# Late stores on SyncE, and spectral-gradient groups between the rows of x's gradient

## The chip, the cores and the metric

The kernel runs on one core of one Trainium2 chip. The metric is the device time of one execution in microseconds (us), the median of several runs. "The span" is the stretch from the first to the last record of one profiled execution. The names of the profile: PE is TensorE (its matmuls; PEld are its weight loads), DVE is VectorE, ACT is ScalarE, POOL is GpSimd, SP is SyncE. A trailing q (SPq, POOLq) means the engine's instruction queue, which also issues transfers.

## The reference

Forward and backward pass of one block in bfloat16, with x of 2048 x 448: a spectral layer, then a token-mixing MLP, each behind a layernorm and with a residual.

```python
h  = x + irfft2(rfft2(layernorm(x)) * (w_r + 1j * w_i))
z  = layernorm(layernorm(h))
h2 = h + (gelu(z.T @ w1 + b1) @ w2 + b2).T
# returned: h2, and for grad_out the gradients of x, w_r, w_i, w1, b1, w2, b2
out_0 = h2
out_1, out_2, out_3 = grad_x, grad_w_r, grad_w_i      # 2048x448, 2048x225, 2048x225
out_4, out_5 = grad_w1, grad_b1                       # 2048x1792, 1792
out_6, out_7 = grad_w2, grad_b2                       # 1792x2048, 2048
```

## The kernel before

The sequence (2048) is cut into 16 rows of 128 partitions, the hidden size F (1792) into 14 blocks of 128. The Fourier transforms are matmuls with tables, with sums and differences on DVE between them.

The program is not written in its final order. Every operation is given to a planner (`Plan.op`) with the engines that may run it, a cost, the buffers it reads and writes, and a level (`pl.boost`). `Plan.order` then places the operations engine by engine: of those that can start it takes the one with the highest priority (the longest chain behind it plus the level). Buffers come from rings of fixed depth; `w4` (5 deep) holds the output rows of out_4 and out_6, `k1` (8) small tiles such as gx, `hx` (3) the loaded rows of x, `e4` (3) the products of the spectral gradients, and `ps` the 8 PSUM banks, of which each kind of use may hold a limited number (`mm` 4, `sb` 4, `mw` 8). Loads on SP have a fixed order. A store (`st`, line 513; its DMA is line 515) goes to POOL unless `on="S"` puts it on SP; an operation waits in its engine's queue, in order, until its data are there.

What is at work in the last 60 us:

- Rows of x's gradient, h = 0 to 15. `ifft_rows` (line 966) makes a row of the inverse transform: four matmuls of `ab` with `di` (tile ps_sb), an ACT copy `odd`, two DVE operations `eo` (lines 977, 979), three matmuls with `kinv` (a "kinv triple"), an ACT copy and two DVE operations `y` (lines 992, 994). `norm_back` (line 1249) is the backward layernorm: a DVE row total (line 1262) and `nm` (line 1274), an ACT `v` (line 1267), DVE `junk` (line 1285) and `gx` (line 1288). Line 1373 stores gx to out_1.
- Outer products of out_6 (14 of them), then of out_4 (16, h = 0 to 15): `outer` (line 1379) makes four banks with 12 whole-array matmuls and four half-array matmuls, the "tails", which run two at a time. Up to `EARLY` (line 1377) the kind is `mm`, with the tails between the second and third bank; from there on the kind is `mw`, with the tails last for even h and first for odd h, so that neighbours share a change of array shape. `copy` evicts each bank as a CAST into `s` (line 523 on ACT, line 525 on DVE). Line 1437 stores a row of out_4 (448 KB); the last row is stored in four pieces of 112 KB (line 1441).
- The spectral gradients out_2 and out_3, in five groups (`JG`, of 4, 3, 3, 3 and 3 planes). `cmul` (line 887) makes two products `t_r` and `t_i` (line 896) and two sums into `ds` (lines 903, 905), all on DVE, and four stores follow. A soft dependency (line 1426) keeps a group's products behind the gx of a given row.

Of the kernel before, what the change touches and what calls it, by code (L numbers as in the profile page):

```python
# [18 lines left out]
P = 128  # L19
S = 2048  # L20
D = 448
DF = 225
F = 1792
# [360 lines left out]
def _act(n, base=0.045):  # L384
    return base + 0.855e-3 * n, base + 0.11 + 0.855e-3 * n
# [6 lines left out]
def on_act(n, base=0.045):  # L392
    return [("ACT", *_act(n, base))]


def on_dve(n, per=1.04e-3, base=0.066):
    return [("DVE", *_dve(n, per, base))]
# [14 lines left out]
def evict(n):  # L412
    return on_act(n) + on_dve(n)


def mm(*cols):
    t = sum(0.002 + 0.4215e-3 * max(n, 120) for n in cols)
    return [("PE", t, t + 0.07)]
# [3 lines left out]
def kernel(  # L422
# [40 lines left out]
    pl = Plan(nc, tc, rings)  # L463
# [14 lines left out]
    def big(i, shape, name, dtype=BF16):  # L478
        return pl.buf(f"X{i}", shape, name, dtype)

    def k1(shape, name, dtype=BF16):
        return pl.buf("k1", shape, name, dtype)

    def bank(kind, shape, dtype=F32):
        return pl.buf("ps", shape, "ps_" + kind, dtype, kind)
# [27 lines left out]
    def st(out, in_, size, r, w=(), issue=0.6, on="P", order=None, rate=0.335):  # L513
        def go(e, on):
            e.dma_start(out=out() if callable(out) else out, in_=in_())  # L515

        pl.op([("POOL", issue, issue) if on == "P" else ("SP", 0.45, 0.45)], go, r=r, w=w,
              dma=(size, rate * 1e6, False), order=order)

    def copy(alts, out, in_, r, w):  # L520
        def go(e, on):
            if on == "ACT":
                e.copy(out=out(), in_=in_())  # L523
            else:
                e.tensor_copy(out=out(), in_=in_())

        pl.op(alts, go, r=r, w=w)

    def matmuls(bk, calls, r, cost=None, modes=("whole", "cols")):


        def go(e, on):
            for n, out, lhsT, rhs, start, stop in calls:
                out, lhsT = out(), lhsT()
                if not split or op.mode != "cols":
                    e.matmul(out, lhsT=lhsT, rhs=rhs(), start=start, stop=stop)  # L536
                    continue
                m, each = out.shape[0], int(np.prod(lhsT.shape[2:]))
                for a, b_ in ((0, 64), (64, m)):
                    e.matmul(out[a:b_], lhsT=lhsT[:, a // each:b_ // each], rhs=rhs(), start=start, stop=stop)  # L540

        split = cost is None
        op = pl.op(cost or mm(*[c[0] for c in calls]), go, r=r, w=bk if isinstance(bk, list) else [bk], modes=modes)
        return op

    def rows(ap):
        return ap.rearrange("(q h) d -> q h d", h=NT)
# [339 lines left out]
    def cmul(a, b, out, j0, j1, conj):  # L887
        n = j1 - j0
        js = range(j0, j1)
        t_r = pl.buf("e4", [P, 2, n, DF], "t_r")  # L890
        t_i = pl.buf("e4", [P, 2, n, DF], "t_i")
        ra = [(a, j) for j in js]
        rb = [(b, j) for j in js] if b is not w_now[0] else [b]

        def times(t, c):
            pl.op(tt(2 * n * DF), lambda e, on: e.tensor_tensor(
                out=t[:], in0=a[:, :, j0:j1, :], in1=b[:, c:c + 1, j0:j1, :].broadcast_to([P, 2, n, DF]),
                op=ALU.mult), r=ra + rb, w=[t])

        times(t_r, 0)  # L900
        times(t_i, 1)
        (o_r, o_i), ow = out(j0, j1)
        pl.op(tt(n * DF), lambda e, on: e.tensor_tensor(out=o_r(), in0=t_r[:, 0], in1=t_i[:, 1],
                                                       op=ALU.add if conj else ALU.subtract), r=[t_r, t_i], w=ow(0))
        pl.op(tt(n * DF), lambda e, on: e.tensor_tensor(out=o_i(), in0=t_r[:, 1], in1=t_i[:, 0],
                                                       op=ALU.subtract if conj else ALU.add), r=[t_r, t_i], w=ow(1))
# [3 lines left out]
    def in_place(b):  # L910
        def out(j0, j1):
            return (((lambda: b[:, 0, j0:j1, :]), (lambda: b[:, 1, j0:j1, :])),
                    lambda c: [(b, (c, j)) for j in range(j0, j1)])
        return out
# [201 lines left out]
    for j in range(NFB):  # L1116
        wc, o = w1c[j]
# [31 lines left out]
        if j % 4 == 3 or j == NFB - 1:  # L1149
            j0 = j - j % 4  # L1150
# [186 lines left out]
    hlnT = big(1, [P, 4, S], "hlnT")  # L1337
    du_t = big(8, [P, 4, F], "du_t")
# [17 lines left out]
    ds = big(4, [P, 2, NJ, DF], "ds")  # L1356
# [7 lines left out]
    gx_op = []  # L1364
    for h in range(NT):
        with grouped():
            py = ifft_rows(ab2, di1, h, y2)
            g = h // 2
            gx = k1([P, D], "gx")
            norm_back((y2, h % 7), lambda g=g, h=h: xr[g][:, h % 2, :], (xr[g], h % 2), h, nx,  # L1370
                      lambda h=h: dh[:, h, :], lambda gx=gx: gx[:], ((dh, h), gx))
        gx_op.append(pl.ops[-1])
        st(rows(out_1[0])[:, h, :], lambda gx=gx: gx[:], P * D * 2, [gx])

    behind, EARLY = [], 10

    def outer(kind, a_t, b_t, j, width, dst, turn, evict_):


        bs = [bank(kind, [P, width]) for _ in range(4)]
        held = [(dst, ("held", 0))]
        begins = (lambda n: n < 2) if turn is None else (lambda n: turn == 0)

        def call(n, rows_, c, start, stop):
            return (width, lambda: bs[n][:], lambda: a_t[rows_, c, j * P:(j + 1) * P],
                    lambda: b_t[rows_, c, width * n:width * n + width], start, stop)

        def whole(*ns):  # L1390
            return matmuls(bs[ns[0]:ns[-1] + 1], [call(n, slice(0, P), c, c == 0 and begins(n), c == 2 and not begins(n))
                                                  for n in ns for c in range(3)],
                           [(a_t, (0, i)) for i in range(4)] + [(b_t, (0, n)) for n in ns] + held)

        def tails():
            return matmuls(bs, [call(n + i, (LO, UP)[i], 3, not begins(n), begins(n)) for n in (0, 2) for i in range(2)],
                           [(t, k) for t in (a_t, b_t) for k in (1, 2)] + held, mm(width, width), ("rows",))

        with grouped():
            if turn is None:  # L1400
                os = [whole(0), whole(1), tails(), whole(2), whole(3)]
            elif turn == 0:
                os = [whole(0, 1), whole(2, 3), tails()]
            else:
                os = [tails(), whole(0, 1), whole(2, 3)]
            for o in os:
                if behind:
                    o.soft.add(behind[-1].idx)
                behind.append(o)
            for n in range(4):  # L1410
                copy(evict_, lambda n=n: dst[:, width * n:width * n + width], lambda n=n: bs[n][:], [bs[n]], [(dst, n)])
                pl.ops[-1].level = 300.0

    for j in range(NFB):
# [2 lines left out]
        st(out_6[j * P:(j + 1) * P, :], lambda s6=s6: s6[:], P * S * 2, [s6],  # L1417
           on="S" if j in s6_at else "P", order=s6_at.get(j))

    pl.boost = 0.0  # L1420
    o23 = [o.rearrange("(q b r) k -> b q r k", b=2, r=NJ) for o in (out_2, out_3)]
    for i, (j0, j1) in enumerate(JG):
        at = len(pl.ops)
        cmul(ds, xs, in_place(ds), j0, j1, True)
        for o in pl.ops[at:at + 2]:
            o.soft.add(gx_op[(3, 6, 9, 12, 15)[i]].idx)
        for c in range(2):
            for b_ in range(2):
                st(o23[c][b_, :, j0:j1, :], lambda c=c, b_=b_, j0=j0, j1=j1: ds[64 * b_:64 * b_ + 64, c, j0:j1, :],
                   64 * (j1 - j0) * DF * 2, [(ds, (c, j)) for j in range(j0, j1)], on="S")  # L1430

    pl.boost = 0.0
    for h in range(NT):
        s4 = pl.buf("w4", [P, F], "s4")
        outer(*(("mm",) if h < EARLY else ("mw",)), hlnT, du_t, h, 448, s4, None if h < EARLY else h % 2, on_act(448) if h < 13 else evict(448))
        if h < NT - 1:
            st(rows(out_4)[:, h, :], lambda s4=s4: s4[:], P * F * 2, [s4])
        else:
            for n in range(4):
                sl = slice(448 * n, 448 * n + 448)  # L1440
                st(rows(out_4)[:, h, sl], lambda s4=s4, sl=sl: s4[:, sl], P * 448 * 2, [(s4, n)], on="SPSP"[n])

# [36 lines left out]
```

## Time and profile before

| | |
|---|---|
| median of 3 runs | 340.83 us (340.62 to 341.41) |
| profiled execution: its own time / its span | 340.38 us / 338.49 us |
| granted TensorE clock over the span | 0.987 |
| PE, DVE, ACT, POOL busy | 95%, 79%, 61%, 17% of the span |
| first matmul of out_4 / last matmul's end | 280.06 us / 329.69 us |
| stores issued after 300 us by POOL / SP | 19 / 22 |

Times are counted from the start of the span. An operation's busy time on DVE or ACT overlaps the next one's by some 0.1 us, so a queue of operations is summed by the differences of their starts. A transfer is seen twice: when its engine issues it, and when its landing is counted by a semaphore.

### The profile page before, as it was taken

How to read it: one execution, taken by the hardware profiler on the slowest of the kernel's cores; microseconds unless marked ns; L12 is line 12 of the kernel's file. 1: busy time of each engine (PE TensorE's matmuls, PEld its weight loads, DVE VectorE, ACT ScalarE, POOL GpSimd, SP SyncE). 2: the span in 40 equal slices, each digit the busy share in tenths (PEclk: the TensorE clock that was granted, in tenths of full speed). 3: DMA queues.
4: the chain of work that ended last, by engine and by line, in shares of the span. 5: the costliest groups of instructions: out<-in, count | busy, mean ns of one | idle time of the engine just before them, and what ended most of it. 6: DMA issues, size and time to landing. Idle time of an engine off the chain costs nothing.

```text
span 338.5 us, 6989 instructions
## 1 busy us (share of the span) xinstructions
PE 321.5 (95%) x2543; PEld 175.3 (52%) x2554; DVE 268.2 (79%) x763; ACT 206.4 (61%) x458; POOL 57.1 (17%) x99
## 2 busy tenths in 40 slices
PE   6869999999999999999999999999999999999990
PEld 2537755666655555555555555554555544544440
DVE  5996999898849997062147988789989799999990
ACT  3886744477668774262302222597877899899650
POOL 0000000047530101042150000000001122433320
PEclk9989999999999999999999999999999999999996
DMA  7999899996698999999999999999982245654684
GB/s 232 383 216 231 180 224 252 209 276 210 200 336 216 338 343 253 282 267 306 269 242 241 257 213 227 229 247 260 266 269 115 103 179 220 244 195 186 220 290 147
DMA packets 135807, 81.01 MB, mean 239 GB/s; under 512 B 94396, under 2 KB 128508, under 8 KB 135644
## 3 DMA queue, kind: packets, MB, share of 16 engines
q1 hardware_dynamic: 129708, 57.70, 73.3%
q0 software_dynamic: 6064, 22.85, 18.7%
q8 instruction: 20, 0.33, 0.4%
q14 instruction: 15, 0.12, 0.1%
HBM read 30.98 MB, written 27.08 MB: 172 GB/s over the span
## 4 chain that ended last, share of the span: by engine, by line
PE 68%; DVE 21%; issue 3%; ACT 2%; DMA 2%; SPq 0%; POOL 0%; POOLq 0%; DVEq 0%; ACTq 0%
PE ps_mp L536 25%; PE ps_mm L536 15%; PE ps_mg L536 10%; PE ps_sp L536 6%; PE ps_sb L536 5%; DVE junk L1262 4%; PE ps_mw L536 4%; DVE junk L1285 4%; PE ps_mm L540 2%; DMA w2n<-in_B_w_dram 2%; ACT v L1267 2%; DVE gg L853 2%; DVE u L806 1%; DVE w L806 1%; DVE bs_x L717 1%
## 5 line engine op out<-in xcount | busy, mean ns | idle before, releaser
L523 ACT CAST s<-ps_mm 128x512 bf16<-128x512 f32 (+1 forms) x96 | 50.3, 582 | 6.2 <-PE ps_mm L536 5.3
L536 PE MATMUL ps_mm<-du,w1T 128*128 128x449 bf16 x224 | 43.4, 353 | 0.0
L536 PE MATMUL ps_mp<-hln,w1c 128*128 128x448 bf16 x224 | 42.9, 352 | 0.0
L536 PE MATMUL ps_mp<-gT,w2c 128*128 128x448 bf16 x224 | 42.9, 352 | 0.0
L536 PE MATMUL ps_mm<-goT,g_t 128*128 128x512 bf16 (+1 forms) x180 | 40.0, 380 | 0.9 <-issue 0.5
L536 PE MATMUL ps_mg<-go_n,w2T 128*128 128x448 bf16 x180 | 40.7, 364 | 0.0
L1267 ACT ACTIVATE v<-ps_mm,nm,rn_h 128x448 f32<-128x448 f32 x16 | 11.6, 725 | 41.0 <-DVE nm L1280 41.0
L536 PEld LDWEIGHTS <-w1T 128*128 128x128 bf16 x224 | 21.7, 97 | 21.0
L536 PEld LDWEIGHTS <-w2c 128*128 128x128 bf16 x224 | 21.9, 98 | 20.5
L536 PEld LDWEIGHTS <-w1c 128*128 128x128 bf16 x224 | 21.9, 98 | 20.3
L536 PEld LDWEIGHTS <-hlnT 128*128 128x128 bf16 (+1 forms) x256 | 19.5, 97 | 21.3 <-issue 6.7
L536 PE MATMUL ps_mm<-du_t,hlnT 128*128 128x448 bf16 (+1 forms) x160 | 30.4, 353 | 0.0
L536 PEld LDWEIGHTS <-w2T 128*128 128x128 bf16 x180 | 16.4, 100 | 13.3 <-issue 2.2
L536 PEld LDWEIGHTS <-g_t 128*128 128x128 bf16 (+1 forms) x191 | 13.3, 97 | 17.0 <-issue 6.0
L1224 DVE SCALAR_TENSOR_TENSOR h<-ps_mp,b2c,hr 128x448 bf16<-128x448 f32 x16 | 9.9, 678 | 14.4 <-PE ps_mp L536 13.8
L515 POOL DMA_DIRECT2D out_dram<-s x25 | 13.5, 542 | 45.0 <-ACT s L523 26.8
L1132 DVE SCALAR_TENSOR_TENSOR ge<-ge 128x448 bf16<-128x448 bf16 x14 | 8.7, 621 | 13.4 <-ACT ge L1130 13.4
L1128 ACT ACTIVATE ge<-ps_mp,b1c 128x448 bf16<-128x448 f32 x14 | 8.8, 626 | 14.1 <-PE ps_mp L536 12.8
L536 PE MATMUL ps_mw<-du_t,hlnT 128*128 128x448 bf16 (+1 forms) x96 | 16.7, 353 | 0.0
L1262 DVE CUSTOM_DVE_ANT_0 junk<-v,hln 128x448 bf16<-128x448 f32 x16 | 10.0, 623 | 7.8 <-ACT v L1267 7.7
L515 POOL DMA_DIRECT2D hn_d<-x x4 | 2.4, 589 | 75.2 <-DVE rn_h L732 71.4
L1231 ACT ACTIVATE gb2j<-go_r 128x448 bf16<-128x448 bf16 x16 | 9.2, 576 | 9.5 <-DMA go_r<-in_grad_out_dram 9.1
(156 smaller groups left out, 634.8 us busy)
## 6 DMA issues: line engine op xcount, KB each, us to landing
w2c<-in_B_w_dram SPq DMA_DIRECT2D x8, 896.0 KB, 9.9
out_dram<-s POOLq DMA_DIRECT2D x15, 448.0 KB, 2.9
w1c<-in_B_w_dram SPq DMA_DIRECT2D x6, 1024.0 KB, 11.9
out_dram<-s POOLq DMA_DIRECT2D x8, 512.0 KB, 3.0
out_dram<-s SPq DMA_DIRECT2D x6, 512.0 KB, 4.5
x<-in_A_x_dram SPq DMA_DIRECT2D x4, 448.0 KB, 7.0
go_n<-in_grad_out_dram SPq DMA_DIRECT2D x2, 896.0 KB, 10.6
hn_d<-x POOLq DMA_DIRECT2D x4, 448.0 KB, 5.2
```

The costliest lines, as they stand in the source:

```text
L515: e.dma_start(out=out() if callable(out) else out, in_=in_())
L523: e.copy(out=out(), in_=in_())
L536: e.matmul(out, lhsT=lhsT, rhs=rhs(), start=start, stop=stop)
L540: e.matmul(out[a:b_], lhsT=lhsT[:, a // each:b_ // each], rhs=rhs(), start=start, stop=stop)
L806: pl.op(tt(4 * n), lambda e, on: e.tensor_tensor(out=out(), in0=in0(), in1=in1(), op=op), r=r, w=w_)
L1128: gop([("ACT", 0.516, 0.62)], [pu, b1c], [uf], lambda e, g, j=j, pu=pu: e.activation(out=g(uf), in_=pu[:, 0:D], func=ACT.Identity, bias=b1 ...
L1132: gop(stt, [q_, uf], [zz], lambda e, g: e.scalar_tensor_tensor(out=g(zz), in0=g(q_), scalar=6.0 * GELU_C, in1=g(uf), op0=ALU.add, op1=ALU. ...
L1224: pl.op([("DVE", 0.595, 0.68)], lambda e, on, t=t, p2=p2, h2=h2: e.scalar_tensor_tensor(out=h2[:], in0=p2[:, 0:D], scalar=b2c[:, t:t + 1], ...
L1231: pl.op([("ACT", 0.70, 0.80)], lambda e, on, h=h: e.activation(out=gb2j[:], in_=go_r[:, h, :], func=ACT.Copy, accum_out=gb2[:, h:h + 1]), ...
L1262: pl.op([("DVE", 0.605, 0.73)], lambda e, on: e.tensor_tensor_reduce(out=junk[:], in0=src(), in1=xhat(), scale=scale(), scalar=0.0, op0=AL ...
L1267: pl.op([("ACT", 0.53, 0.64)], lambda e, on: e.activation(out=v[:], in_=rowsum(), func=ACT.Identity, scale=nm.rn[:, h, 0:1], bias=ab[:, 1:2]),
L1285: pl.op([("DVE", 0.595, 0.68)], lambda e, on: e.scalar_tensor_tensor(out=junk[:], in0=xhat(), scalar=by(), in1=v[:], op0=ALU.mult, op1=ALU ...
```

## The change

- gx rows 0 to 11 go to POOL as before, rows 12 to 15 to SP.
- Rows 0 to 7 of out_4 go to POOL, rows 8 to 14 and all four pieces of row 15 to SP (before: POOL, and the pieces alternately on SP and POOL).
- The stores of the first three groups of ds go to POOL, those of the last two to SP (before: all to SP).
- The groups get a level of 20 (before: none) and may start behind the gx of rows 2, 5, 8, 10 and 13 (before: 3, 6, 9, 12, 15).
- The first 13 outer products of out_4 are of kind `mm` (before: 10), and ACT alone evicts the first 14 (before: 13).

```diff
-        st(rows(out_1[0])[:, h, :], lambda gx=gx: gx[:], P * D * 2, [gx])
+        st(rows(out_1[0])[:, h, :], lambda gx=gx: gx[:], P * D * 2, [gx], on="P" if h < 12 else "S")
...
-    behind, EARLY = [], 10
+    behind, EARLY = [], 13
...
-    pl.boost = 0.0
+    pl.boost = 20.0
...
         cmul(ds, xs, in_place(ds), j0, j1, True)
         for o in pl.ops[at:at + 2]:
-            o.soft.add(gx_op[(3, 6, 9, 12, 15)[i]].idx)
+            o.soft.add(gx_op[(2,5,8,10,13)[i]].idx)
...
-                   64 * (j1 - j0) * DF * 2, [(ds, (c, j)) for j in range(j0, j1)], on="S")
+                   64 * (j1 - j0) * DF * 2, [(ds, (c, j)) for j in range(j0, j1)], on="P" if i < 3 else "S")
...
-        outer(*(("mm",) if h < EARLY else ("mw",)), hlnT, du_t, h, 448, s4, None if h < EARLY else h % 2, on_act(448) if h < 13 else evict(448))
+        outer(*(("mm",) if h < EARLY else ("mw",)), hlnT, du_t, h, 448, s4, None if h < EARLY else h % 2, on_act(448) if h < 14 else evict(448))
...
-            st(rows(out_4)[:, h, :], lambda s4=s4: s4[:], P * F * 2, [s4])
+            st(rows(out_4)[:, h, :], lambda s4=s4: s4[:], P * F * 2, [s4], on="P" if h < 8 else "S")
...
-                st(rows(out_4)[:, h, sl], lambda s4=s4, sl=sl: s4[:, sl], P * 448 * 2, [(s4, n)], on="SPSP"[n])
+                st(rows(out_4)[:, h, sl], lambda s4=s4, sl=sl: s4[:, sl], P * 448 * 2, [(s4, n)], on="S")
```

## The prediction

> **What bounds the kernel now.** I first read the table of engines and the chain that ended last on the page: TensorE (PE) is busy 95% of the span.
>
> ```profile
> PE 321.5 (95%) x2543; PEld 175.3 (52%) x2554; DVE 268.2 (79%) x763; ACT 206.4 (61%) x458; POOL 57.1 (17%) x99
> ...
> PE 68%; DVE 21%; issue 3%; ACT 2%; DMA 2%; SPq 0%; POOL 0%; POOLq 0%; DVEq 0%; ACTq 0%
> ```
>
> The order of instructions of the two programs is the same up to about 278 us, so only the end matters. The windows of that end (columns: stretch, length, busy time and count of each engine, granted clock, DMA share, GB/s):
>
> ```profile
> 297.00:302.00 5.00, 4.91 (x36) 2.44 (x35) 5.00 (x17) 4.87 (x12) 1.62 (x3) 1.00 0.46 156
> ...
> 322.00:327.00 5.00, 5.00 (x32) 2.40 (x30) 4.93 (x9) 2.25 (x6) 1.08 (x2) 1.00 0.91 306
> 327.00:332.00 5.00, 2.69 (x16) 1.09 (x12) 2.78 (x6) 2.20 (x5) 1.63 (x3) 1.00 0.89 296
> ```
>
> PE and VectorE (DVE) are both full to 327 at clock 1.00. PE ends at 329.69, yet the span ends at 338.49: 8.80 us without arithmetic. The timeline of the last 14 us and the rows of the closing line 1476 show what fills them:
>
> ```profile
> 324.63 7.10 SPq L515 DMA_DIRECT2D out_dram<-ds  x9
> 324.77 4.92 PE L536 MATMUL ps_mw<-du_t,hlnT 128*128 128x448 bf16 x28
> ...
> 329.73 0.62 DVE L525 CAST s<-ps_mw 128x448 bf16<-128x448 f32 x1 [0.46 <-PE ps_mw L536]
> 330.65 0.54 POOL L515 DMA_DIRECT2D out_dram<-s  x1 [0.54 <-DVE s L525]
> 331.83 1.01 SPq L515 DMA_DIRECT2D out_dram<-s  x2
> ```
>
> ```profile
> L1476 POOLq EVENT_SEMAPHORE  x4: 17/17/17, 337.8 to 338.4; - x4
> L1476 POOLq DRAIN  x3: 40/93/7094, 330.6 to 338.2; - x3
> L1476 SPq DRAIN  x3: 7/7/50, 335.7 to 338.0; - x3
> ```
>
> Two queues are late. SyncE (SP) still issues stores of ds at 331.1 although DVE wrote their data at 328.6, and it sees the last landing at 334.84 and is done at 335.80. GpSimd (POOL) issues its last store from 330.65 to 331.19, and its closing DRAIN of 7.09 us ends at 337.72; only then does it release the others (337.77) and the span ends 0.73 us later. So POOL's drain ends the span, and SP's queue is next, 1.9 us before it.
>
> **PE, part by part.** Both orders hold the same matmuls and the same shapes. What differs is the number of changes between whole-array and half-array matmuls: three more outer products of out_4 (10 to 12) are of the kind with the half-array tails in the middle, so two changes each, where rows paired in turn shared one. Counted in the orders it is 4 more. In the trace each of the 28 changes after 277 us costs 0.092 to 0.099 us over the 0.189 us slot of a 448-column matmul: 4 x 0.094 = +0.38 us. Against that stand PE's waits for DVE. Laid end to end, before's PE stream from the first matmul of out_4 (280.06) comes to 328.31; it really ended at 329.53 (start of the last plus 0.189), 1.22 late. DVE lays the same way: starts 0.30 apart for y, eo and gx, 0.60 for the row total and for junk, 0.14 for nm, 0.77 and 0.42 for a product and a sum of a 675-element group (1.00 and 0.53 for the 900 one), 0.53 for a cast. From row 2's gx at 278.88 this sum puts row 11's gx at 313.51; the trace has 313.39. So the method holds. Now each kinv triple of PE must come after its eo: before, the latest eo stands 1.05 us behind PE's own sum (the last one, 308.18 against 307.13), in the changed order 0.91 (307.84 against 306.93). After the last kinv (eo ready at 319.3, PE's sum 318.5) nothing holds PE. PE's sum ends at 328.69 in the changed order; with a lateness of 1.0 to 1.2 it ends at 329.7 to 329.9: +0.2 us. I take 329.9 for 329.69.
>
> **DVE and ACT.** DVE does the same work less one 0.53 us cast (outer 13 goes to ScalarE (ACT) whole). From 279.18 its 13 rows and 5 groups are 47.3 us: 326.45. Row 15 adds one bare round trip nm, ACT v, junk, which costs 0.76 us (v's row) plus two handoffs, say 0.95, since nothing stands between them any more: 327.4. Then four casts, the first two of outer 14, whose banks PE closes at about 329.9 - 2.74 = 327.2 (14 slots and one change). They end at 328.5 to 328.6. ACT's extra cast (0.47) lies in its idle time before 321.3 and 326.8 (1.06 and 2.64 us); without that cover it would be paid in full.
>
> **POOL.** It loses four gx stores, seven s stores and the two last pieces, and gains 12 ds stores: 32 late stores for 33. No ds store ran on POOL. Its price is bounded by the 0.542 us of every store of s and the 0.754 us of the du_d store; I take 0.54 to 0.75, 6.5 to 9.0 us, beside 35 us in which POOL idled since 278. Behind them wait stores of s, whose five-deep ring asks for a slot back only five outer products (14 us) later. What counts is that POOL's last store (row 11) leaves at about 316, so its 7.1 us drain is over by 324, beside PE's work. It is worth 1.9 us at once: then SP ends the span.
>
> A sentence of the Trainium skill says otherwise (VectorE: DVE Perf Modes, The DRAIN you can't avoid): the closing DRAINs are put at some 12 ns each on all five engines. SP's here agree (7 ns), POOL's does not (7094 ns); by that sentence nothing of the 1.9 us would come, and the gain would be SP's alone, 0.9 us.
>
> **SP.** It loses 12 ds stores and gains seven s stores, four gx stores and two pieces. Its late queue is: four ds of the last group (DVE's sum gives them at 323.85), gx 14, outer 13, gx 15 (327.6), outer 14 (328.6), four pieces of outer 15 (the last one cast at 329.9 + 0.04 + 0.62 = 330.6). Issues of a 448 KB store took 0.53 to 0.64, of ds 0.47 to 1.19. If all are ready in time and cost 0.58 with the gap, the last piece starts at 328.65 + 4 x 0.58 = 331.0. Before's mean from 319.7 to 332.8 was 13.2 / 18 = 0.73 per issue; 11 of those behind 323.85 give 331.9. I take 331.4. From the start of a 112 KB piece to its landing were 2.37 and 2.70 us: 333.9. From landing to SP's last DRAIN were 0.95 us, to POOL's release 0.1, to the end 0.73: 335.7.
>
> Against the change stands the Trainium skill, DMA: Bandwidth & Descriptors (Issuing engines are not separate DMA queues): it says that a second issuing engine saves only the time to initiate, usually small. By it alone, moving stores between SP and POOL gives nothing, and putting four pieces on one queue costs two issues more, 1.1 us.
>
> **The sum.** Span 338.49 to 335.7: -2.8 us (-1.9 drain, -1.1 SP's queue, +0.2 PE). The profiled execution took 340.38, 1.9 more than its span, so 337.6; the median of the runs is 340.83, 0.45 above it, and I forecast 338.0 from the median. Its own range is 337.3 to 339.0 (issues of 0.58 to 0.75, PE ending at 329.5 to 330.4).
>
> **Rivals.** *SP becomes the bound* (0.10). The 12 late issues stand in one queue and slow each other while the 16 DMA engines are 0.9 busy; for it are ds issues of 0.86, 1.11 and 1.19 us. At 0.86 each the last starts at 333.3, the span ends at 337.6: 339.9. Against it: 12 ds stores have left the end, so there are fewer packets.
>
> *The drain does not go* (0.05). It stays until the landings of all queues are over, or is no cause of the end. For it: its end (337.7) lies 3 us behind the last landing, on any queue. Against: it began while SP was still issuing. Then only SP's part is gained (336.6, which is 335.80 + 0.1 + 0.73, less 335.7): 340.83 - 0.9 = 339.9. This is also what the Trainium skill's 12 ns would make of it.
>
> *PE waits behind the groups* (0.08, the slower side). Before, one product stood among the rows, at 284.96, and next to it PE waited 0.34 us for an eo. Now five whole groups stand there: 3.06 + 4 x 2.38 = 12.6 us of DVE. PE takes its matmuls in order, so an eo behind a group holds all outer products behind its kinv. From 2.8 of the 12.6 us on the gain is gone; with half exposed (6.3) it is 340.83 - 2.8 + 6.3 = 344.3. Against: in the changed order 6.1 to 7.4 us of PE's own work stand between the kinv triples around each of the first four groups, the fifth comes after the last triple, and the lateness is 0.91, as above.
>
> The change does what it says: the orders show no POOL store behind row 11's.
>
> **How the numbers follow.** Forecast 0.77, the rivals 0.10, 0.05, 0.08. A difference of 0.2% (0.7 us) is what a measurement of this kernel can tell. The forecast and the two small-gain rivals are faster, but their tails reach into no change by 0.05: faster 0.87, same 0.05, slower 0.08. The range takes in PE without lateness (-0.9) and the two small-gain rivals: 336.8 to 340.0.
>
> **What would show it.** Right: POOL's long DRAIN lies well before the last matmul; SP's last store starts at 331 to 332 and the span ends some 4.3 us later; PE's last matmul ends within 0.5 us of 329.7; DVE has no idle time above 0.5 us but the one before row 15's junk. Wrong: PE waits for eo of over 1 us in all between 280 and 320, SP issues still back to back after 332, or a POOL DRAIN that ends behind SP's.

## The result, and the profile after

The changed kernel takes 335.86 us (median of four runs, 335.25 to 336.96) against 340.92 us before: the ratio is 0.9854, with a 95% interval of 0.9826 to 0.9882. It is faster, and by more than forecast: -5.1 us where -2.8 was said, and below the range (336.8 to 340.0). The profiled execution took 335.88 us with a span of 334.1 us.

The page's rows of engines and of the chain: the share of PE grows, and POOL has left the chain.

```profile
PE 323.8 (97%) x2554; PEld 176.2 (53%) x2554; DVE 267.7 (80%) x762; ACT 207.1 (62%) x459; POOL 56.3 (17%) x98
...
PE 70%; DVE 23%; ACT 3%; issue 2%; DMA 1%; DVEq 0%; ACTq 0%
```

The windows of the end (same columns as before): PE is still full to 327 and DVE no longer is; POOL does nothing behind 322; the DMA engines' share between 322 and 327 fell from 0.91 to 0.55.

```profile
297.00:302.00 5.00, 5.00 (x40) 2.60 (x39) 5.00 (x17) 4.78 (x13) 1.87 (x4) 1.00 0.68 238
322.00:327.00 5.00, 5.00 (x30) 2.44 (x32) 4.04 (x11) 3.52 (x8) 0.00 (x0) 1.00 0.55 174
327.00:332.00 5.00, 2.87 (x18) 1.14 (x14) 3.00 (x6) 1.99 (x4) 0.00 (x0) 1.00 0.86 310
```

The timeline of the last 10 us, the last line of POOL's own timeline, and the rows of the closing line:

```profile
324.76 5.11 PE L536 MATMUL ps_mw<-du_t,hlnT 128*128 128x448 bf16 x29
...
326.70 0.69 DVE L1285 SCALAR_TENSOR_TENSOR junk<-xr,nm,v 128x448 bf16<-128x448 bf16 x1 [0.89 <-ACT v L1267]
...
328.94 2.47 SPq L515 DMA_DIRECT2D out_dram<-s  x5
...
329.91 0.62 DVE L525 CAST s<-ps_mw 128x448 bf16<-128x448 f32 x1 [0.50 <-PE ps_mw L536]
```

```profile
316.06 0.54 POOL L515 DMA_DIRECT2D out_dram<-gx  x1 [6.30 <-DVE gx L1288]
```

```profile
L1476 POOLq EVENT_SEMAPHORE  x4: 17/17/17, 333.4 to 334.0; - x4
L1476 POOLq DRAIN  x3: 40/93/7009, 316.0 to 333.8; - x3
L1476 SPq DRAIN  x3: 7/7/13, 333.3 to 333.6; - x3
```

PE's last matmul ends at 329.87 (329.69 before). POOL's long DRAIN is as long as before, but it runs from 316.04 to 323.05, beside the matmuls. SP issues its last store at 331.02, sees it land at 332.92, and is done at 333.36; POOL releases the others 0.03 us later. So SP ends the span, 4.24 us behind PE, where POOL ended it 8.80 us behind PE.

How much of the 5.1 us belongs to the change? Up to the first matmul of out_4 PE's two orders hold the same work, except four small matmuls (0.19 us) that stood ahead of it before. From the same point on, before needs 338.49 - 279.87 = 58.62 us and the changed kernel 334.12 - 279.56 = 54.56: **-4.06 us**. The body ahead of it took 279.87 and 279.56 us here, and over all profiles below that stretch's first matmul began anywhere from 278.8 to 280.9. Before's profiled execution was also 0.5 us below its own median.

### The profile page after: what moved, and what is told of

Same layout as the page of the kernel before. It is cut to its first block, busy times and chain, and to the rows that moved or that the text cites. A ratio compares the mean times of both kernels' runs of the same rounds, so it can differ in the third digit from the quotient of the medians.

```text
span 334.1 us, 7003 instructions
## 1 busy us (share of the span) xinstructions
PE 323.8 (97%) x2554; PEld 176.2 (53%) x2554; DVE 267.7 (80%) x762; ACT 207.1 (62%) x459; POOL 56.3 (17%) x98
## 4 chain that ended last, share of the span: by engine, by line
PE 70%; DVE 23%; ACT 3%; issue 2%; DMA 1%; DVEq 0%; ACTq 0%
PE ps_mp L536 25%; PE ps_mm L536 17%; PE ps_mg L536 10%; PE ps_sp L536 6%; PE ps_sb L536 5%; DVE junk L1262 4%; DVE junk L1285 3%; DVE bs_x L717 3%; PE ps_mw L536 3%; PE ps_mm L540 2%; ACT v L1267 2%; DVE gg L853 2%; DVE u L806 1%; DVE w L806 1%; DVE go_r L1288 1%
## 5 line engine op out<-in xcount | busy, mean ns | idle before, releaser
L523 ACT CAST s<-ps_mm 128x512 bf16<-128x512 f32 (+1 forms) x108 | 56.3, 580 | 6.2 <-PE ps_mm L536 5.4
L536 PE MATMUL ps_mm<-goT,g_t 128*128 128x512 bf16 (+1 forms) x191 | 41.0, 380 | 0.0
L536 PE MATMUL ps_mg<-go_n,w2T 128*128 128x448 bf16 x180 | 39.9, 359 | 0.0
L536 PE MATMUL ps_mm<-du_t,hlnT 128*128 128x448 bf16 (+1 forms) x208 | 39.2, 353 | 0.0
L536 PEld LDWEIGHTS <-kinv 128*128 128x128 bf16 x144 | 11.3, 98 | 6.7 <-DVE eo L979 2.5
L1267 ACT ACTIVATE v<-y,nm,rn_x 128x448 f32<-128x448 f32 x16 | 12.3, 771 | 3.8 <-DVE nm L1274 3.8
```

Source lines behind the costliest of these rows:

```text
L1267: pl.op([("ACT", 0.53, 0.64)], lambda e, on: e.activation(out=v[:], in_=rowsum(), func=ACT.Identity, scale=nm.rn[:, h, 0:1], bias=ab[:, 1:2]),
```

## The experiments

The theory: the gain is POOL's closing DRAIN, which no longer ends the span; then SP's queue, which the groups of ds had jammed. One rival: the drain is harmless, and the new order of the groups brings the gain. A second question came with the result: why is the tail shorter still than predicted?

**The pieces back on two queues (e1).** Edit on the changed kernel:

```diff
-                st(rows(out_4)[:, h, sl], ..., [(s4, n)], on="S")
+                st(rows(out_4)[:, h, sl], ..., [(s4, n)], on="SPSP"[n])
```

> The changed kernel with two of the four last pieces (second and fourth) on POOL, so that POOL again issues a store after the last matmul. Theory of the drain (POOL's closing DRAIN lasts 6.5 us behind the end of its last issue and holds the end): last cast ends at about 330.4, POOL issues to about 331.1, drain to 337.6, span 338.3, +4.2 against the changed kernel's 334.1, so the gain over the kernel before is all but gone (-0.2). Rival (the drain is no cause; the gain came from ds leaving SP's late queue): SP has two issues fewer, span 333.3 to 334.1, gain 4.4 to 5.2 kept.

Ratio 1.0028 (1.0004 to 1.0053): the gain is gone, and a little more. Rows of the closing line, and POOL's timeline:

```profile
L1476 POOLq DRAIN  x3: 40/93/7172, 331.6 to 339.3; - x3
L1476 SPq DRAIN  x3: 7/7/13, 334.9 to 339.1; - x3
```

```profile
330.55 0.54 POOL L515 DMA_DIRECT2D out_dram<-s  x1 [13.11 <-DVE s L525]
331.67 0.54 POOL L515 DMA_DIRECT2D out_dram<-s  x1 [0.58 <-DVE s L525]
```

SP is done at 335, POOL's drain runs from 331.65 to 338.82. Two stores of 112 KB on POOL cost 4.6 us: from the first matmul of out_4 to the end it is 59.19 us, in the changed kernel 54.56. The rival falls.

**The queues alone (e2)**: the kernel before with the four changed `on=` and nothing else.

> The kernel before with the new queues of all stores and nothing else; the orders of PE, DVE and ACT are those of before. Theory of the drain: POOL's last store (ds of the third group) leaves at about 324, its drain is over by 331; SP then has eight ds, outer 14 and four pieces behind 326, last issue at 331.8, landing 2.0 later, end 1.2 behind that: span 335.0, -3.5 us. Rival (the gain comes from the new order of the groups): 338 or so, within 0.7 us of before.

Ratio 0.9917 (0.9891 to 0.9943), span 336.16. From the first matmul of out_4 it needs 56.33 us where before needs 58.43: -2.1, between the two expectations and less than the -3.5 of the theory. The drain is over at 331.45, as expected; the tail is SP's. POOL's row, and the timeline of SP, which shows what is in its way:

```profile
L1476 POOLq DRAIN  x3: 40/93/7832, 323.6 to 335.9; - x3
```

```profile
325.58 4.01 SPq L515 DMA_DIRECT2D out_dram<-ds  x6
329.70 0.53 SPq L515 DMA_DIRECT2D out_dram<-s  x1
330.33 1.11 SPq L515 DMA_DIRECT2D out_dram<-ds  x2
331.54 2.03 SPq L515 DMA_DIRECT2D out_dram<-s  x4
```

The last groups of ds are still made at 325 to 328.6 in this order, so their eight issues stand ahead of the pieces, and the last piece leaves at 333.18 where 331.8 was expected.

**The order alone (e3)**: the changed kernel with all stores on the queues of before.

> The changed kernel's order, EARLY, level and evictions with the stores on the queues of before. Theory of the drain: POOL issues the last piece to about 331.1, drain to 337.6, span 338.3, no gain (-0.2). Rival (order): most of the 4.4 us is kept, span near 334.5.

Ratio 1.0011 (0.9987 to 1.0035): nothing gained, as the theory of the drain said.

```profile
L1476 POOLq DRAIN  x3: 40/93/7094, 331.3 to 338.9; - x3
L1476 SPq DRAIN  x3: 7/7/13, 334.8 to 338.7; - x3
```

The order alone brings SP forward and leaves the end to POOL, and it costs PE 0.5 us. Queues alone are worth 2.1 us, the order alone loses 0.5 (59.11 against 58.62), both together gain 4.1: the order's 2.0 us can be had only once the drain is out of the way.

**A late POOL instruction that is no store (e4).** Added to the changed kernel:

```diff
+    pl.op([("POOL", 0.1, 0.2)], lambda e, on, s4=s4: e.tensor_copy(out=warm[:], in_=s4[:, F - 1:F]), r=[(s4, 3)], w=[warm])
```

> The changed kernel with one more POOL instruction at the very end: a copy of one column of the last output tile, which waits for the last cast (about 330.4); no store more on POOL. If the long DRAIN is what POOL pays behind any late instruction: POOL to 330.7, drain to 337.2, span 338, +4. If it is paid for stores issued by POOL only, and those are over by then: span 334.1, within 0.3.

Ratio 0.9986 (0.9959 to 1.0013). POOL's timeline, then its closing row (line 1477 here):

```profile
317.24 0.54 POOL L515 DMA_DIRECT2D out_dram<-gx  x1 [6.30 <-DVE gx L1288]
331.78 0.18 POOL L1444 CAST warm<-s 128x1 f32<-128x1 bf16 x1 [14.00 <-DVE s L525]
```

```profile
L1477 POOLq DRAIN  x3: 40/102/6671, 331.8 to 338.9; - x3
```

A copy of 0.18 us, with POOL's last store 14 us behind it, pays the drain in full: it ends at 338.43, 6.46 us behind the copy and 4.4 us behind the last landing of a store (334.04). So the drain is no waiting for landings. It follows POOL's last instruction, a copy as well as a store.

**All groups on POOL (e8)**: `on="P"` for all five groups.

> The changed kernel with the stores of all five groups on POOL. POOL's last store then ends at about 326.0 in place of 316.6. If the closing DRAIN is 6.5 to 7.1 us behind POOL's last instruction, it ends at 332.5 to 333.1, just ahead of SP (333.3): the span stays within 0.3 us of the changed kernel's. If the drain also waits for landings of other queues or grows with stores just issued, it ends behind 333.5 and the span grows by as much.

Ratio 0.9896 (0.9866 to 0.9926). POOL's last issue ends at 326.48, the drain at 333.67, SP's second DRAIN is at 333.61: the two queues are level, and from PE's end to the span's end it is 4.27 us (4.24 in the changed kernel). The drain is 7.2 us behind the last issue here, and 7.1 in e2; both times a store of ds was last. Behind a store of 128 partitions it was 6.45 to 6.6 us. What makes the difference was not taken apart: a ds store has 64 partitions, and it is also the fourth of four issued back to back.

**EARLY back at 10 (e5).**

> The changed kernel with EARLY back at 10, all else as changed. If the only price is the changes of array shape (0.094 us each, two fewer in this order): PE ends 0.2 us earlier, ratio to the changed kernel 0.999, span -0.2. By the end-to-end sums: the last kinv triple stands behind outer products of kind mw that run before it, its eo is 1.96 us late against PE's sum (0.91 in the changed kernel), so PE waits about 1 us more and the span is 0.7 to 0.9 us longer than the changed kernel's, about 335.

Ratio 0.9909 (0.9874 to 0.9944), an interval that overlaps the changed kernel's; the traces tell them apart. PE's stretch of out_4 takes 52.31 us in place of 50.31, the whole end 1.4 us more. PE's waits from 279 to 333 us (waited for, us in total, times, longest):

```profile
PE ps_mw L536 <- ACT s L523: 1.0, 2, 0.7
PE ps_sb L536 <- DVE eo L979: 0.2, 1, 0.2
PE ps_sb L536 <- ACT s L523: 0.2, 1, 0.2
```

In the changed kernel only the last of these lines is there. The lateness of eo showed that this would go wrong, but not its size: 0.9 us was expected, and most of the 2.0 us is mw banks that wait for ACT's eviction (1.0 us as PE's idle time above, 1.6 us by the differences of starts). With all else as changed, the later switch to kind mw is thus worth 1.4 us, which the forecast had only as a price of 0.38.

**The tail: three pieces, a halved last bank, EARLY 12 (e6, e7, e9).** e6 stores banks 0 and 1 of the last row together; e7 adds an eviction of the last bank half by ACT, half by DVE; e9 is e7 with EARLY 12.

```diff
-            for n in range(4):
-                sl = slice(448 * n, 448 * n + 448)
+            for a, b_ in ((0, 2), (2, 3), (3, 4)):
+                sl = slice(448 * a, 448 * b_)
...
```

> The changed kernel with row 15 of out_4 stored in three pieces, the first of two banks. The last store starts about 0.7 us behind PE's end in place of 1.15. If the landing is a fixed 1.9 us: PE's end to the span's end 3.8 in place of 4.24. If the data of rows 14 and 15 are still under way (the halved last bank gained nothing): 4.1 to 4.2, the landing taking 2.2 to 2.3.

> The changed kernel with the last row of out_4 stored in three pieces (the first of two banks) and the last bank evicted half by ACT and half by DVE. If the end is set by SP's queue behind PE: the last cast ends 0.27 us earlier and the last store starts at 330.35 in place of 331.02, PE's end being the same; from PE's last matmul to the span's end 0.65 us less, span 333.4 for a body like that of the changed kernel's profile. If the last landing were set by the data (bandwidth), within 0.2 us.

> The kernel of the halved last bank with EARLY 12: two changes of array shape fewer, the kinv triples as late as in the changed kernel (0.91 at most). Sum: 0.65 for the tail, 0.19 for PE: span 0.8 us below the changed kernel's, ratio to the kernel before about 0.983. Rival: the tail is set by landings, then 0.2 at most.

None gains. e6, like e12 below, ran once (335.38 and 335.59 us), so the two are read by their traces alone. In e6 the last store leaves 0.69 us behind PE's end in place of 1.15, SP sees it land 2.27 us later in place of 1.90, and PE's end to the span's end is 4.26 us (e7: 4.24, ratio 0.9892, 0.9864 to 0.9921). e7's halves came out one behind the other, so the last data were ready later (0.81 us behind PE's end, 0.66 in the changed kernel), not earlier as planned. e9 has 54.54 us from the first matmul of out_4 to the end, the changed kernel 54.56 (ratio 0.9882, 0.9854 to 0.9910). Its PE needs 50.49 us, 0.18 more than the changed kernel where 0.19 less was expected: at 323.14 a half-array matmul of kind mw starts 0.21 us late, released by an ACT eviction. The sum of -0.65 was wrong twice: it had the two halves end together, and it took the landing for a fixed price.

**Is the landing a matter of data? (e12, e11)** e12 is e6 without the store of row 14. e11 makes row 14 bank by bank and stores it in two halves.

> The kernel of the three pieces without the store of row 14 of out_4 (448 KB; that row of the output is not written). If the last landing waits for the data of rows 14 and 15 on the 16 DMA engines: the landing falls from some 2.2 to 1.8 us and PE's end to the span's end to 3.7. If the price from issue to landing is fixed: no change against the three pieces.

> The changed kernel with row 14 of out_4 made bank by bank (tails first, row 13 with tails last, as many changes of array shape), stored in two halves, and row 15 stored in three pieces. If the last 0.9 MB are what the end waits for: 224 KB leave about 1 us earlier, the last store starts 0.7 us behind PE's end in place of 1.15, and from PE's end to the span's end it is 3.7 us in place of 4.24. If the landing is a fixed price: 3.8 by the earlier start alone. If SP's queue is in the way (one issue more, behind gx of row 15): 4.2 or more.

Windows of the last microseconds, e6 first, then e12 (the last two columns are DMA share and GB/s):

```profile
330.00:331.00 1.00, 0.00 (x0) 0.00 (x0) 0.02 (x1) 0.00 (x0) 0.00 (x0) 1.00 0.96 364
331.00:332.00 1.00, 0.00 (x0) 0.00 (x0) 0.00 (x0) 0.00 (x0) 0.00 (x0) 1.00 0.72 246
```

```profile
330.00:331.00 1.00, 0.00 (x0) 0.00 (x0) 0.39 (x1) 0.00 (x0) 0.00 (x0) 1.00 0.83 294
331.00:332.00 1.00, 0.00 (x0) 0.00 (x0) 0.00 (x0) 0.00 (x0) 0.00 (x0) 1.00 0.50 165
```

With row 14's 448 KB gone, the last piece lands 1.69 us behind its issue in place of 2.27. With row 14's halves leaving 3.05 and 2.14 us ahead of PE's end (e11), where the whole row left 0.93 ahead in e6, it is 1.72, and the tail behind PE shrinks to 3.62 us, as expected. So what the landing has above some 1.7 us, which no run goes below, is data still under way: in e6 the engines move 0.9 MB in the three microseconds from 329. The DMA packets of the traces show the same, for the kernel before too. A piece of 112 KB is 128 packets of 896 B; for the last 128 such packets of SP's stores, in us behind the start of the last issue (SP sees the landing 0.01 to 0.09 us later):

```
kernel    first packet starts  last packet ends  landing
before           1.25               1.99           2.36
changed          1.01               1.42           1.88
e2               0.90               1.35           1.76
e6               1.38               1.82           2.19
e11              0.84               1.31           1.70
e12              0.84               1.30           1.67
```

The landing follows the last packet by 0.36 to 0.45 us each time; what differs is when the packets' turn comes. In before they also take 0.74 us to pass, elsewhere 0.41 to 0.47, and why was not taken apart.

The end of e12 gained less (4.10) because one step of 0.41 us stands in SP's closing waits, where the steps beside it take 0.07, without a visible cause. Such a step stands there in before, e1, e3 and e12 and is seen in no other kernel, where a wait for a landing may hide it; what it is stays open. e11 paid its gain back: row 14 waits 0.41 us for a bank in mid-row, PE needs 50.91 us in place of 50.31, and the total is 54.52. Its ratio is 0.9876 (0.9835 to 0.9916). No version beat the changed kernel clearly.

**The changed kernel again (e10).**

> The changed kernel once more, beside the kernel before on the same chip. In all kernels with its order so far PE needed 50.31 us from its first matmul of out_4 to its last, and the start of that stretch lay anywhere from 279.2 to 280.9. If the excess of the first measurement (5.1 us) over the 4.0 us of the stretch and the tail was such a shift of the body: ratio 0.988, about 336.6. If it belongs to the change: 0.985 again.

336.05 us, ratio 0.9862 (0.9830 to 0.9894), an interval that holds both expected values. PE's stretch, the drain and the tail repeat to within 0.1 us (50.31, 6.45, 4.21). The six kernels whose stretch from out_4's first matmul to the end is 54.5 to 54.6 us have ratios of 0.985, 0.986, 0.988, 0.988, 0.989 and 0.990. Their mean, 0.988, is 4.2 us: close to the 4.06 that the traces show as the change's own. The rest of the 5.1 lies within the spread of the body, which no experiment took apart.

The kernels in one table (us; the first column from the first matmul of out_4 to PE's end):

```
kernel        PE's stretch  PE's end to span's end  last POOL work ends  its drain ends
before            49.63            8.80                  331.19             337.72
changed           50.31            4.24                  316.60             323.05
e1                50.31            8.88                  332.21             338.82
e2                49.64            6.69                  324.32             331.45
e3                50.31            8.80                  331.87             338.40
e4                50.31            8.16                  331.97             338.43
e5                52.31            3.64                  317.62             324.07
e8                50.30            4.27                  326.48             333.67
e11               50.91            3.62                  315.85             322.30
```

## Why the prediction was right in kind and wrong in size

- *The drain* was right: out of the way by 323.05, 10 us ahead of the last landing, and then SP ends the span. e2, with the order of before, gains 2.1 us (1.9 in the sum, though e2 moves SP's stores too); e1 and e3 give the gain back with the late stores. The prediction tied the drain to POOL's last store; e4 shows that a late copy pays it too. The rival "the drain does not go" fell.
- *PE, +0.2 us* was a little low. From the same point the stretch grew by 0.49 us (50.31 against 49.63 + 0.19). The four changes of array shape are there (32 against 28 after 277 us). The waits for eo are 0.52 us in all (0.60 before), close to the sum of latenesses, and one wait of 0.25 us at 304.38, for a DVE `y` that ends at 304.32, was not in it. That PE's end came out as forecast (329.87 for 329.9) is luck: the body ahead started the stretch 0.31 us earlier.
- *DVE* came as worked out: gx of row 15 starts at 327.42, and the one bare round trip shows as 0.89 us of idle time. The rival of *PE behind the groups* fell: no eo made PE wait for more than 0.38 us.
- *POOL* came as worked out: its ds issues took 0.53 to 0.54 us each, the low end of 0.54 to 0.75, and its last store left at 316.06.
- *SP's last issue*, 331.4, was 331.02. The middle between 0.58 and 0.73 per issue was the wrong choice: row 14's store left at 328.94 (328.65 in the sum) and the five last issues start 0.52 apart. The ds issues of 0.86 to 1.19 us that raised the 0.73 do not come back: none of the changed kernel takes over 0.60. Why they got shorter was not taken apart. The rival *SP becomes the bound* came true only in that SP ends the span; its price did not.
- *From the last issue to the end*, 4.3 us, was 3.1, and this is the step that failed. Landing: 2.54 us in the sum, 1.90 measured. Closing waits to POOL's release: 1.05 in the sum, 0.47 measured. Both had been read off before's tail and carried over as fixed prices, although the change takes the ds stores and POOL's late stores out of that tail. e6, e11 and e12 show the landing between 1.69 and 2.27 us by the data under way, and the packets show it for the two kernels themselves; of the closing waits, some 0.33 us is the long step whose cause is open (0.40 in before, in place of 0.07).

The windows behind the last issue (332.47 before, 331.02 in the changed kernel), before first, show how long the engines stay full (the last three columns are granted clock, DMA share and GB/s):

```profile
332.00:333.00 1.00, 0.00 (x0) 0.00 (x0) 0.00 (x0) 0.00 (x0) 0.00 (x0) 0.97 0.86 248
333.00:334.00 1.00, 0.00 (x0) 0.00 (x0) 0.00 (x0) 0.00 (x0) 0.00 (x0) 0.50 0.90 296
```

```profile
331.00:332.00 1.00, 0.00 (x0) 0.00 (x0) 0.00 (x0) 0.00 (x0) 0.00 (x0) 1.00 0.96 321
332.00:333.00 1.00, 0.00 (x0) 0.00 (x0) 0.00 (x0) 0.00 (x0) 0.00 (x0) 1.00 0.40 132
```

In before they stay near 0.9 busy until 1.5 us behind the last issue, in the changed kernel until 1.0 us. The last two ds stores of before, issued at 330.55 and 331.14, land only at 333.97 and 334.21, so their data are among those ahead of the last piece. How much of the difference is theirs and how much is that of POOL's late pieces, no run takes apart.

The terms add up: -0.4 for the issue, -0.65 for the landing and -0.6 for the closing are the 1.6 us between the span forecast (335.7) and found (334.1); PE's +0.3 and the body's -0.3 stand inside the first and cancel. The rest of the miss, some 0.5 us from 338.0 to 335.86, is in the step from span to median: the forecast put the median 0.45 above the profiled execution, as it was before, and the changed kernel's lies level with it. The range had bounds for PE and for the issues, but none for the landing and the closing, nor for the body's spread of some 2 us. Its lower end, 336.8, is 1.2 us below 338.0, not the 0.9 named for it: 1.2 is what lies between PE's forecast end (329.9) and its sum without lateness (328.69).

## What to carry to other kernels

Look behind the last matmul: when POOL does anything late, a store or a copy of 0.18 us, its closing drain ends 6.5 to 7.2 us behind that and can be the end of the kernel (in e8, with POOL's last issue over 3.7 us ahead of PE's end, the two queues were level). So give POOL's late work to a queue that closes quickly, and take all of it, since one late copy costs 3.9 of the 4.1 us (e4) and two late pieces all of it (e1). Once that is gone the last queue in order is the next bound, so work that ends in stores has to be made earlier, not only stored elsewhere (e2 against the changed kernel). A price that was read in a crowded tail, the time to a landing above all, is not the price in the tail that the change leaves.

## What the runs showed of the hardware

- POOL's closing DRAIN ends 6.45 to 6.6 us behind its last instruction where that is a store of 128 partitions, 6.46 behind a copy with POOL's last store 14 us earlier, 7.1 to 7.2 behind a ds store of 64 partitions. SP's last 7 to 50 ns; ACT's and DVE's first one 0.56 and 0.66 us, their second 14 and 19 ns. The 12 ns of the Trainium skill (VectorE: DVE Perf Modes, The DRAIN you can't avoid) are near SP's and these second ones, and far from POOL's long one.
- The last piece of 112 KB on SP lands 1.69 (e12) to 2.8 us (e1) after its issue starts, by what else is under way; where that piece is the last to move, its landing is 0.36 to 0.45 us behind its last packet. The 16 engines moved up to 376 GB/s in a microsecond of the changed kernel's tail, at a share of 0.97.
- The order of PE's instructions fixes its time closely: 50.30 or 50.31 us in the changed kernel, e1, e3, e4, e8 and e10, which share it, while the body ahead of it varied by 2 us from run to run.
